# A linear-attention and gMLP block: k^T v regrouped as (x^T k) Wv, accumulated while tokens arrive, with some first layernorms on ScalarE and another order of loads

## The chip, the core and the metric

The kernel runs on one NeuronCore of a Trainium2 chip. The metric is the device time of one execution in microseconds, lower is better. Beside it stand profiles: each is one profiled execution, with the span from its first to its last instruction.

## What is computed

One token sequence, S = 2048 tokens of D = 512 channels in bf16, passes through two blocks:

```python
h  = x + A(layernorm(x))          # linear attention, 32 heads of 16 channels
h2 = h + B(layernorm(h))          # gMLP, F = 1792, Fh = 896

# A: q, k, v = x @ wqkv;  phi(t) = (t + 1 if t > 0 else exp(t)) + 1e-6
kv  = einsum('bhsd,bhse->bhde', phi(k), v);   z = einsum('bhsd->bhd', phi(k))
o   = (phi(q) @ kv) / (phi(q) . z + 1e-6);    A = o @ wo
# B: z1, z2 = halves of gelu(x @ w_in)
g   = w_sp @ layernorm(z2) + b_sp;            B = (z1 * g) @ w_out
```

Only the products of channels within one head count in kv, so the 512 x 512 product of phi(k) and v is masked to blocks of 16. Since v = x Wv for the normalised x, the product k^T v can also be written by way of x^T k and Wv.

## The kernel before

The 2048 tokens are 16 tiles of 128 (NT), taken in 8 pairs (NP). Everything stays in SBUF. The eight PSUM banks (2 KB per partition each) are handed out by a pool, `PS`, one bank or an aligned run of banks at a time; a pool slot is free again when the last operation on its tile has ended.

The program is a list of operations (`op`), each with an engine, a planned cost, a priority and the operands that it reads and writes. `Program.schedule` (L185) plays this list through with the planned costs and fixes the order of each engine's queue and the buffer slots: each engine takes the operation that could start soonest, within a small patience, and among those the one of the lowest priority number. `NUDGE` (L372) is a table of numbers added to the priorities, one for each operation. At run time the order of each queue (PE, ACT, DVE, POOL, SP) is fixed, with semaphore waits where `_waits` (L274) found a dependence. DMAs are issued by the queues of SP, ACT and POOL; on POOL each DMA also waits until the one before it has landed.

The stages, by line:

- Loads (L539 to L552): tile 0 by SP, tile 1 by ACT, wk in two halves, the other tiles in pairs, wv and wq by SP. wo, win and wout by POOL: wo after tile 5 is normalised (L657), wout after the q projections of L743 (L744), win after the seventh pair's phi(k) (L719). w_sp is transposed by DMA on SP's queue as time permits (L554), 26 of 64 pieces early.
- Warm-up of PE: eight matmuls on zeros (L603), in a PSUM bank of their own.
- First layernorm (L643): statistics (L610, L614) on DVE, the root by Ln and Exp on ACT (L624, L626), the normalisation on DVE (L638) into a pool of four tiles, `XN`.
- Transposes of the normalised tiles into xT: pairs 0 to 2 on PE (L676) with an evacuation by ACT (L681), the others by DMA on SP's queue (L665). `XDMA` = 3 is that border.
- For each pair the projections k and v (L708, each 8 matmuls of 512 columns into two banks). phi(k): Exp on ACT (L687), min on DVE (L688), max on DVE (L695), into pk. v: evacuated by ACT (L722), beside two columns of ones.
- q projections (L734) for groups of four tiles, with the same phi, into pqT. The fourth group comes after the tokens (L857).
- k^T v (L757): for each of four channel blocks 16 matmuls of 130 columns, accumulated over the token tiles; the columns of ones give z. Then on DVE a copy of z (L769), the mask (L775) and a transpose (L777). The product with wo (L787) is evacuated by DVE and ACT (L795, L792) into mw.
- Denominators (L807 to L814), their spreading (L824, L846) and scaling of pqT (L850), then y = pq mw (L879), the residual (L884), the second layernorm.
- Stage B: win (L907 for z2, L952 for z1), the token mixing (L982) and the output projection (L1000), all on PE.

Of the kernel before, what the change touches and what calls it, by code (L numbers as in the profile page):

```python
# [5 lines left out]
FP32 = mybir.dt.float32  # L6
# [103 lines left out]
class Program:  # L110
# [293 lines left out]
def bass_sequential_preLN__linear_attn_block__mixer_gmlp__prompt_kernel(  # L404
# [18 lines left out]
    VS = 136  # L423
# [20 lines left out]
    pk_b, v_b = NT * D * 2, NT * KD * VS * 2  # L444
    s_kv = Store(nc, "pk_v_z2", pk_b + v_b)
    s_xn = Store(nc, "xn", 4 * D * 2)
# [17 lines left out]
    v = View(s_kv, pk_b, [NT, KD, VS], BF16)  # L464
    gz2 = View(s_kv, 0, [NT, FH], BF16)
    mw = View(s_kv, NT * FH * 2, [KD, D], BF16)

# [20 lines left out]
    mhalf = small([TPG], FP32)  # L488

# [7 lines left out]
    xn_v = View(s_xn, 0, [4, D], BF16)  # L497
# [43 lines left out]
    load("act", "x1", x[1, :], x_dram[P:2 * P, :], P * D * 2, prio=-20)  # L541
    for c in (0, 2):
        load("sp", "wk", wk[c:c + 2, :], w3[:, c:c + 2, D:2 * D], D * D + (170000 if c == 0 else 0), whole=True, prio=c / 2 + 1)

    def load_x(p, prio):
        load("sp", f"x{p + 1}", x[2 * p:2 * p + 2, :],
             x_dram[2 * p * P:(2 * p + 2) * P, :].rearrange("(n p) d -> p n d", p=P), 2 * P * D * 2, prio=prio)

    for p in range(1, NP):
        load_x(p, 2 + p)  # L550
    load("sp", "wv", wv.all(), w3[:, :, 2 * D:3 * D], D * D * 2, prio=2.5 + WV)
    load("sp", "wq", wq.all(), w3[:, :, 0:D], D * D * 2, prio=2 + NP)  # L552

    def load_wsp(tg, sts, after=()):  # L554
# [186 lines left out]
    for gq in range(NQ1):  # L741
        for f in (0, 2):
            o = q_proj(gq, f, Q0 - 5 + gq)  # L743
# [331 lines left out]
```

## Time and profile before

| | us |
|---|---|
| median of 3 runs | 253.16 (252.9 to 253.57) |
| the profiled execution's own time | 253.07 |
| its span | 251.3 |
| PE busy, share of the span | 240.3, 96% |
| DVE busy | 137.4, 55% |
| ACT busy | 82.1, 33% |
| POOL busy | 24.5, 10% |

In the profile PE is TensorE's matmuls, PEld its weight loads, DVE is VectorE, ACT is ScalarE, POOL is GpSimd, SP is SyncE; a q behind the name is the engine's queue of DMA issues. L12 is line 12 of the kernel. A group gives its line, engine, operation, output<-inputs, shapes, count, then busy time, mean time of one in ns, idle time of the engine just before, and who ended it. Buffers that share a store have one name: xT_pq_z is xT, pqT and z1T; pk_v_z is phi(k), v, mw and z2; wqkv_wsp is wq, wk, wv, wo and later part of w_sp. [...]

### The profile page before, as it was taken

To read this page: it belongs to the slowest core of one execution; us is meant where nothing else is said; L and a number is where in the kernel's file an instruction comes from. 1 tells how busy PE (TensorE), PEld (TensorE's weight loads), DVE (VectorE), ACT (ScalarE), POOL (GpSimd) and SP (SyncE) were. 2 spreads that over 40 slices of the span, in tenths; PEclk is the share of its full clock that TensorE was granted. 3 is DMA by queue.
4 is the path that set the end of the run, shared out by engine and by line. 5 is a ranking of instruction groups with operands and counts; after the bars stand their busy time and mean duration, and the time that the engine had idled before them with its cause. 6 is when DMAs were issued, how large, how long until landed. Compare 5 with 4: busy or idle time off the path is not lost.

```text
span 251.3 us, 3084 instructions
## 1 busy us (share of the span) xinstructions
PE 240.3 (96%) x1204; PEld 110.7 (44%) x1204; DVE 137.4 (55%) x265; ACT 82.1 (33%) x115; POOL 24.5 (10%) x65
## 2 busy tenths in 40 slices
PE   5879989998999999999999999999999999999995
PEld 1434434473344444444444444444444444444442
DVE  2888897677999989905233223343313523323443
ACT  3638456638965666686920000000010000000000
POOL 7300000110020352412300000000000000000000
PEclk9999999999999999999999999999999999999999
DMA  6994644799301230435444444211000110000022
GB/s 196 357 220 104 93 99 104 188 234 257 100 5 36 42 69 17 86 84 93 97 105 103 87 104 104 63 41 45 0 0 3 42 42 0 0 3 0 0 83 83
DMA packets 54782, 21.30 MB, mean 85 GB/s; under 512 B 48400, under 2 KB 54032, under 8 KB 54768
## 3 DMA queue, kind: packets, MB, share of 16 engines
q1 hardware_dynamic: 53968, 17.71, 31.7%
q0 software_dynamic: 656, 3.28, 4.1%
q8 instruction: 9, 0.15, 0.3%
q10 hardware_dynamic: 144, 0.13, 0.2%
q14 instruction: 5, 0.04, 0.1%
HBM read 7.47 MB, written 2.10 MB: 38 GB/s over the span
## 4 chain that ended last, share of the span: by engine, by line
PE 84%; DVE 6%; DMA 5%; SPq 2%; ACT 1%; issue 1%
PE ps L982 38%; PE ps L907 10%; PE ps L1000 10%; PE ps L952 10%; PE ps L708 6%; PE ps L734 5%; PE ps L879 4%; DMA wqkv_wsp<-in_A_wqkv_dram 4%; SPq L536 2%; DVE xT_pq_z L695 2%; PE ps L757 1%; DVE xT_pq_z L850 1%; DMA xT_pq_z<-xn 1%; ACT e L687 1%; DVE small L610 1%
## 5 line engine op out<-in xcount | busy, mean ns | idle before, releaser
L982 PE MATMUL ps<-wsp,pk_v_z 128*128 128x512 bf16 x336 | 73.2, 379 | 0.0
L988 DVE TENSOR_TENSOR r<-ps,e 128x512 bf16<-128x512 f32 x28 | 19.4, 691 | 67.5 <-PE ps L982 67.5
L982 PEld LDWEIGHTS ps<-wsp,pk_v_z 128*128 128x128 bf16 x336 | 32.9, 98 | 39.7
L957 ACT ACTIVATE xT_pq_z<-ps 128x1024 bf16<-128x1024 f32 x14 | 14.2, 1023 | 62.1 <-PE ps L952 61.9
L708 PE MATMUL ps<-wqkv_wsp,xT_pq_z 128*128 128x512 bf16 x128 | 29.3, 379 | 0.9 <-ACT xT_pq_z L681 0.5
L907 PE MATMUL ps<-win,hT 128*128 128x512 bf16 (+1 forms) x128 | 25.7, 353 | 0.4 <-ACT hT L681 0.4
L952 PE MATMUL ps<-hT,win 128*128 128x512 bf16 x112 | 25.2, 379 | 0.0
L1000 PE MATMUL ps<-wout,xT_pq_z 128*128 128x512 bf16 x112 | 24.7, 379 | 0.0
L982 PE MATMUL ps<-wqkv_wsp,pk_v_z 128*128 128x512 bf16 x112 | 24.3, 379 | 0.0
L610 DVE BATCH_NORM_STATS2 small<-xh 128x6 f32<-128x512 bf16 x32 | 20.9, 679 | 4.6 <-DMA xh<-in_A_x_dram 4.5
L687 ACT ACTIVATE e<-ps 128x1024 bf16<-128x1024 f32 x16 | 16.1, 1023 | 13.1 <-PE ps L708 8.0
L708 PEld LDWEIGHTS ps<-wqkv_wsp,xT_pq_z 128*128 128x128 bf16 x128 | 12.1, 98 | 16.5 <-ACT xT_pq_z L681 1.2
L907 PEld LDWEIGHTS ps<-win,hT 128*128 128x128 bf16 x128 | 12.4, 98 | 13.0 <-ACT hT L681 0.7
L916 ACT ACTIVATE pk_v_z<-ps 128x896 bf16<-128x896 f32 x16 | 14.5, 915 | 10.9 <-PE ps L907 10.8
L734 PE MATMUL ps<-xT_pq_z,wqkv_wsp 128*128 128x512 bf16 x64 | 15.5, 379 | 2.5 <-DMA wqkv_wsp<-in_A_wqkv_dram 1.6
L1006 DVE TENSOR_TENSOR r<-ps,xh 128x512 bf16<-128x512 f32 x16 | 11.1, 691 | 11.7 <-PE ps L1000 11.7
L982 PEld LDWEIGHTS ps<-wqkv_wsp,pk_v_z 128*128 128x128 bf16 x112 | 11.0, 98 | 13.2
L1000 PEld LDWEIGHTS ps<-wout,xT_pq_z 128*128 128x128 bf16 x112 | 11.0, 98 | 13.2
L952 PEld LDWEIGHTS ps<-hT,win 128*128 128x128 bf16 x112 | 11.0, 98 | 12.8
L879 PE MATMUL ps<-pk_v_z,xT_pq_z 128*128 128x512 bf16 x64 | 15.2, 379 | 0.6 <-DVE xT_pq_z L850 0.5
L931 DVE BATCH_NORM_STATS2 small<-pk_v_z 128x6 f32<-128x512 bf16 (+1 forms) x16 | 9.8, 619 | 9.6 <-ACT pk_v_z L916 9.4
L638 DVE TENSOR_SCALAR xn<-xh,small 128x512 bf16<-128x512 bf16 x32 | 12.0, 408 | 1.9 <-DMA xT_pq_z<-xn 1.2
(68 smaller groups left out, 173.5 us busy)
## 6 DMA issues: line engine op xcount, KB each, us to landing
out_dram<-r SPq DMA_DIRECT2D x16, 128.0 KB, 1.7
xh<-in_A_x_dram SPq DMA_DIRECT2D x7, 256.0 KB, 6.6
win<-in_B_w_in_dram POOLq DMA_DIRECT2D x1, 1792.0 KB, 9.8
wqkv_wsp<-in_A_wqkv_dram SPq DMA_DIRECT2D x2, 512.0 KB, 7.7
wout<-in_B_w_out_dram POOLq DMA_DIRECT2D x1, 896.0 KB, 6.2
wsp<-in_B_w_sp_dram SPq DMA_TRANSPOSE x48, 2.8
wqkv_wsp<-in_A_wqkv_dram SPq DMA_DIRECT2D x2, 256.0 KB, 4.0
wqkv_wsp<-in_A_wo_dram POOLq DMA_DIRECT2D x1, 512.0 KB, 8.8
```

The lines of the kernel that those rows point to most:

```text
L610: op("dve", dve_c(512), lambda e: e.bn_stats(s6.ap(), src.ap()), r=[src], w=[s6], prio=prio)
L687: op("act", act_c(1024), lambda e: e.activation(e_().ap(), t(flat).ap(), ACT.Exp), r=[t()], w=[e_()], prio=prio)
L708: i = e.matmul(t(bank(ti)).ap(), lhsT=lhs.ap()[:, c, :], rhs=rhs.ap()[:, c, :], start=(c == 0), stop=(c == KD - 1))
L734: r_ = e.matmul(t(bank(i)).ap(), lhsT=lhs.ap()[:, c, :], rhs=rhs.ap()[:, c, :], start=(c == 0), stop=(c == KD - 1))
L879: i = e.matmul(t(bank(ti)).ap(), lhsT=l.ap()[:, c, :], rhs=mw[c, :].ap(), start=(c == 0), stop=(c == KD - 1))
L907: k = e.matmul(t(bank(i)).ap()[:, 0:b - a], lhsT=l.ap()[:, c, :], rhs=win[c, a:b].ap(), start=(c == 0), stop=(c == KD - 1))
L916: op("act", act_c(FH, ptr=by_act), lambda e, t=t, d=d, acc={"accum_out": m.ap()} if by_act else {}: e.activation(d.ap(), t(flat).ap()[:, 0 ...
L952: k = e.matmul(t(bank(i)).ap(), lhsT=l.ap()[:, c, :], rhs=r_.ap()[:, c, :], start=(c == 0), stop=(c == KD - 1))
L957: op("act", act_c(1024), lambda e: e.activation(d.ap(), t(None if same else flat).ap(), ACT.Gelu_apprx_tanh), r=[t()], w=[d], prio=prio, a ...
L982: k = e.matmul(t(bank(0)).ap(), lhsT=l.ap()[:, s - a, :], rhs=r_.ap()[:, s - a, :], start=(s == 0), stop=(s == NT - 1))
L988: op("dve", dve_c(512), lambda e: e.tensor_tensor(gb().ap(), t(bank(0)).ap(), bsp().ap()[:, tg * GW:(tg + 1) * GW], ALU.add), r=[t(), bsp( ...
L1000: k = e.matmul(t(bank(0)).ap(), lhsT=l.ap()[:, fc, :], rhs=wout[fc, :].ap(), start=(fc == 0), stop=(fc == KF - 1))
```

## The change

- v is no longer projected. From each tile's normalised x (lhsT) and phi(k) (rhs), four matmuls of 512 columns add to x^T k in four PSUM banks, `acc`, held from the warm-up (which now writes there) to the end of the tokens. Their priority is 10p + `KA`, KA = 35.
- After the tokens x^T k is copied to SBUF (half by ACT, half by DVE), multiplied by Wv (16 matmuls of 128 columns), and masked straight into kvmT; the two DVE transposes go. z comes from 16 matmuls of a block of 32 ones columns with phi(k), on four strips of output columns, a copy by ACT and four matmuls of two columns.
- All 16 normalised tiles have places of their own (`xn`, where v was). Of tiles 4 to 15, those with n % 4 >= `NA` = 1 are normalised by ACT (Identity with scale and bias per partition; DVE makes the bias).
- Tile 1 is loaded by SP after tile 0, then tiles 2 and 3; half of wk by ACT, behind the memset of the warm-up operand; wq after tiles 8 and 9, wv last. wo is loaded after tile 12's normalisation instead of tile 5's.
- Pair 2 is transposed by DMA too (`XDMA` = 2). The first three q groups have priority 20gq + `QI`, QI = 15. `NUDGE` has other numbers throughout.

```diff
-    WARM, XDMA, HDMA, LNACT = 8, 3, 1, 2
-    WV = 2
+    WARM, XDMA, HDMA, LNACT = 8, 2, 1, 2
+    WV, WQ, NA, KA, QE, QI = 8.5, 4, 1, 35, 3, 15
...
-    load("act", "x1", x[1, :], x_dram[P:2 * P, :], P * D * 2, prio=-20)
-    for c in (0, 2):
-        load("sp", "wk", wk[c:c + 2, :], ..., D * D + (170000 if c == 0 else 0), whole=True, prio=c / 2 + 1)
...
+    load("sp", "x1", x[1, :], x_dram[P:2 * P, :], P * D * 2, prio=1)
+    for p in range(1, NP):
         load("sp", f"x{p + 1}", ..., 2 * P * D * 2, prio=1 + p)
+    load_wk = [load(e, "wk", wk[c:c + 2, :], ..., D * D + 60000, whole=True, prio=q)
+               for e, c, q in (("act", 0, -20), ("sp", 2, 2.5))]
+    load("sp", "wv", wv.all(), w3[:, :, 2 * D:3 * D], D * D * 2, prio=1.5 + WV)
+    load("sp", "wq", wq.all(), w3[:, :, 0:D], D * D * 2, prio=1.5 + WQ)
...
-    idle = Tile(PS)
+    acc = Tile(PS, KD)
...
+        by_act = [n for n in grp if n >= 4 and n % 4 >= NA]
+        if by_act:
+            nb = small([len(grp)], FP32)
+            op("dve", 0.11, lambda e, nb=nb, m=m, rs=rs: e.scalar_tensor_tensor(
+                nb.all().ap(), m.ap(), -1.0, rs.all().ap(), op0=ALU.mult, op1=ALU.mult), ...)
         for i, n in enumerate(grp):
+            if n in by_act:
+                o = op("act", act_c(512, ptr=1), lambda e, d=d, n=n, a=a, c=c: e.activation(
+                    d.ap(), x[n, :].ap(), ACT.Identity, bias=c.ap(), scale=a.ap()), ...)
+            else:
+                o = normalise(d, x[n, :], Row(st_x, n), 6, rs[i:i + 1], 10 * (n // 2) - 18)
+            if n == 12:
+                load("pool", "wo", ...).deps[o] = True
...
-        t = kv_proj(p, wv, 10 * p + 1)
-        op("act", act_c(1024), ..., r=[t()], w=[d], prio=10 * p + 1)
+        for n in (2 * p, 2 * p + 1):
+            l, r_ = xn[n, :], pk[n, :]
+            def mm(e, n=n, l=l, r_=r_):
+                for c in range(KD):
+                    i = e.matmul(acc(bank(c)).ap(), lhsT=l.ap()[:, c * P:(c + 1) * P], rhs=r_.ap(), start=(n == 0),
+                                 stop=(n == NT - 1))
+            op("pe", 4 * MM, mm, r=[l, r_], w=[acc()], prio=10 * p + KA)
...
-            o = q_proj(gq, f, Q0 - 5 + gq)
+            o = q_proj(gq, f, 20 * gq + QI if gq < QE else Q0 - 5 + gq)
...
+    zp, zs, zt = Tile(PS), Tile(XN), Tile(PS)
+        for n in range(NT):
+            a = 32 * (n % 4)
+            i = e.matmul(zp(bank(0)).ap()[a:a + 32, :], lhsT=ones.all().ap(), rhs=pk[n, :].ap(), start=(n < 4),
+                         stop=(n >= NT - 4))
...
+    op("act", act_c(512), lambda e: e.activation(zs().ap(), zp(bank(0)).ap(), ACT.Copy), ..., prio=Q0 + 2)
+            i = e.matmul(zt(bank(0)).ap()[:, 2 * c:2 * c + 2], lhsT=zs().ap()[:, c * P:(c + 1) * P], rhs=part.all().ap(), ...)
...
+        if h == 0:
+            op("act", act_c(1024), lambda e, d=d, s=s: e.activation(d.ap(), s.ap(), ACT.Copy), ..., prio=Q0 + 2)
+        else:
+            op("dve", dve_c(1024), lambda e, d=d, s=s: e.tensor_copy(d.ap(), s.ap()), ..., prio=Q0 + 2)
+        for c in range(KD):
+            for j in range(KD):
+                i = e.matmul(vk(bank(0)).ap()[:, c * P:(c + 1) * P], lhsT=wv.ap[:, j, c * P:(c + 1) * P],
+                             rhs=xtk.ap[:, j, c * P:(c + 1) * P], start=(j == 0), stop=(j == KD - 1))
+    op("dve", dve_c(512), lambda e: e.tensor_tensor(kvmT()..., vk(bank(0))..., bmask..., ALU.mult), ..., prio=Q0 + 2)
```

More of the change, by code (lines that the diff above doesn't have):

```diff
@@ L488, in bass_sequential_preLN__linear_attn_block__mixer_gmlp__prompt_kernel @@
     mhalf = small([TPG], FP32)
+    ones = small([32], BF16)
+    part = small([2], BF16)
     psum = nc.alloc_psum_tensor("ps", [P, 8, 512], FP32)
@@ L565, in bass_sequential_preLN__linear_attn_block__mixer_gmlp__prompt_kernel @@
     warm = zeros.all()
-    op("pool", 0.3, lambda e: e.memset(warm.ap(), 0.0), w=[warm], prio=-9)
+    load_wk[0].deps[op("pool", 0.3, lambda e: e.memset(warm.ap(), 0.0), w=[warm], prio=-9)] = True
     op("pool", 0.2, lambda e: e.memset(ident.all().ap(), 0.0), w=[ident.all()])
@@ new lines, in bass_sequential_preLN__linear_attn_block__mixer_gmlp__prompt_kernel, with mm @@
+    zp, zs, zt = Tile(PS), Tile(XN), Tile(PS)
+    def mm(e):
+        for n in range(NT):
+            a = 32 * (n % 4)
+            i = e.matmul(zp(bank(0)).ap()[a:a + 32, :], lhsT=ones.all().ap(), rhs=pk[n, :].ap(), start=(n < 4),
+                         stop=(n >= NT - 4))
+        return i
+    op("pe", 1.1, mm, r=[pk.all(), ones.all()], w=[zp()], prio=Q0 + 1.5)
+    op("act", act_c(512), lambda e: e.activation(zs().ap(), zp(bank(0)).ap(), ACT.Copy), r=[zp()], w=[zs()], prio=Q0 + 2)
+    def mm(e):
+        for c in range(KD):
+            i = e.matmul(zt(bank(0)).ap()[:, 2 * c:2 * c + 2], lhsT=zs().ap()[:, c * P:(c + 1) * P], rhs=part.all().ap(),
+                         start=True, stop=True)
+        return i
@@ new lines, in bass_sequential_preLN__linear_attn_block__mixer_gmlp__prompt_kernel, with sums @@
+    op("pe", 0.25, mm, r=[zs(), part.all()], w=[zt()], prio=Q0 + 2)
+    d = zc[:, 0:HC]
+    def sums(e, d=d):
+        m = bmask.ap.rearrange("p (a h e) -> p a h e", a=1, e=DH)[:, :, :, 0].to_broadcast([P, KD, HC])
+        s = zt(bank(0)).ap()[:, 0:2 * KD].rearrange("p (c f) -> p c f", f=2)[:, :, 0:1]
+        return e.tensor_tensor(d.ap(), m, s.to_broadcast([P, KD, HC]), ALU.mult)
+    op("dve", 0.15, sums, r=[zt(), bmask.all()], w=[d], prio=Q0 + 2)
+    for h in range(2):
+        d = xtk[2 * h:2 * h + 2, :]
+        s = acc(lambda v, h=h: v[:, 2 * h:2 * h + 2, :])
+        if h == 0:
+            op("act", act_c(1024), lambda e, d=d, s=s: e.activation(d.ap(), s.ap(), ACT.Copy), r=[s], w=[d], prio=Q0 + 2)
+        else:
+            op("dve", dve_c(1024), lambda e, d=d, s=s: e.tensor_copy(d.ap(), s.ap()), r=[s], w=[d], prio=Q0 + 2)
@@ new lines, in bass_sequential_preLN__linear_attn_block__mixer_gmlp__prompt_kernel, with mm @@
+    vk, kvmT = Tile(PS), Tile(XN)
+    def mm(e):
+        for c in range(KD):
+            for j in range(KD):
+                i = e.matmul(vk(bank(0)).ap()[:, c * P:(c + 1) * P], lhsT=wv.ap[:, j, c * P:(c + 1) * P],
+                             rhs=xtk.ap[:, j, c * P:(c + 1) * P], start=(j == 0), stop=(j == KD - 1))
+        return i
+    op("pe", 16 * 0.058, mm, r=[wv.all(), xtk.all()], w=[vk()], prio=Q0 + 2)
+    op("dve", dve_c(512), lambda e: e.tensor_tensor(
+        kvmT().ap().rearrange("p (c f) -> p c f", c=KD), vk(bank(0)).ap().rearrange("p (c f) -> p c f", c=KD),
+        bmask.ap.rearrange("p (a f) -> p a f", a=1).to_broadcast([P, KD, P]), ALU.mult),
+       r=[vk(), bmask.all()], w=[kvmT()], prio=Q0 + 2)
```

79 lines of the change are left out of this document (24 added, 55 removed), and 53 rows, old and new, of the table NUDGE.

## The prediction

> **What bounds the kernel now.** I read the first part of the page, then busy time by stretch, the chain that ended last, and TensorE's waits.
>
> ```profile
> span 251.3 us, 3084 instructions
> PE 240.3 (96%) x1204; PEld 110.7 (44%) x1204; DVE 137.4 (55%) x265; ACT 82.1 (33%) x115; POOL 24.5 (10%) x65
> ```
> ```profile
> 0.00:6.58 6.58, 3.60 (x9) 1.04 (x9) 2.05 (x6) 2.06 (x5) 4.74 (x22) 1.00 0.70 201
> 6.58:25.34 18.76, 16.19 (x88) 7.32 (x89) 15.90 (x39) 11.64 (x18) 1.68 (x4) 1.00 0.88 224
> 25.34:50.87 25.53, 24.67 (x113) 10.88 (x114) 20.65 (x33) 14.16 (x16) 0.95 (x1) 1.00 0.59 124
> 50.87:67.32 16.45, 15.07 (x136) 8.00 (x135) 12.91 (x22) 11.16 (x15) 0.79 (x1) 1.00 0.94 216
> 67.32:248.43 181.11, 180.73 (x860) 83.46 (x860) 85.24 (x168) 43.03 (x63) 16.36 (x38) 1.00 0.21 48
> 248.43:251.30 2.87, 0.00 (x0) 0.00 (x0) 0.69 (x1) 0.00 (x0) 0.00 (x0) 1.00 0.27 91
> ```
>
> The columns of the second view are the stretch, its length, then PE, PEld, DVE, ACT, POOL busy, the clock, DMA share, GB/s. From 67.32 to 248.43 PE is busy 180.73 of 181.11 us: that part is solid matmul work, and no line of it is in the diff. So the time is a sum: when PE's real work starts, plus its work, plus its idle time before 67.32, plus fixed parts. Whatever the change does to the moment 67.32 is carried to the end one for one, as long as stage B's inputs keep up. PE's idle time is 2.57 us in the early stretch (18.76 - 16.19), 0.86 in the middle one, 1.38 in the tail.
>
> ```profile
> PE ps L734 <- DMA wqkv_wsp<-in_A_wqkv_dram: 1.6, 1, 1.6
> PE ps L734 <- DVE xT_pq_z L695: 0.7, 1, 0.7
> ```
>
> The largest single wait after the start is L734 (q) for the DMA of wq: 1.6 us, in the early stretch.
>
> **The change part by part.** *PE work.*
>
> ```profile
> 41.37 9.50 PE ps L708 x44
> 52.59 3.63 PE ps L757 x64
> 57.08 0.33 PE ps L807 x4
> 69.22 0.24 PE ps L676 x4
> ```
>
> These are rows of the chain (start, length, what, count). A 512-wide matmul is 9.50 / 44 = 0.216 us. Of L708's 128 matmuls the 64 for v go (13.8 us); x^T k brings 64 of the same width (4 per token tile, 16 tiles): 13.8 us, net nothing. The k^T v block, L757, goes: -3.63. The third pair is transposed by DMA, so 8 PE transposes go: 2 x 0.24 = -0.48. Added: Wv against x^T k, 16 matmuls of 128 columns, at L757's 3.63 / 64 = 0.057: 0.91. Four 2-column matmuls that turn the sums: at most 4 x 0.057 = 0.23. And 16 matmuls of 512 columns on 32 output columns each (the sums of pk). No row shows those sixteen; the nearest is L807, four such matmuls on four different column strips, 0.33 us for the four, where one after another they would take 0.86. Bounds: 4 x 0.216 = 0.86 if the four strips overlap fully, 16 x 0.216 = 3.46 if not at all; I take 1.1, a little under 4 x 0.33. Sum: -3.63 - 0.48 + 0.91 + 0.23 + 1.1 = **-1.87 us**. [...]
>
> *Start.*
>
> ```profile
> 0.80 0.39 SPq L536 DMA_DIRECT2D xh<-in_A_x_dram  x1
> 0.80 0.40 ACTq L536 DMA_DIRECT2D xh<-in_A_x_dram  x1
> 1.23 1.28 ACT L596 ACT_TABLE_LOAD   x1 [1.23 <-PEq L1060]
> 3.82 1.29 DVE L610 BATCH_NORM_STATS2 small<-xh 128x6 f32<-128x512 bf16 x2 [3.82 <-DMA xh<-in_A_x_dram]
> 7.35 1.29 DVE L610 BATCH_NORM_STATS2 small<-xh 128x6 f32<-128x512 bf16 x2 [0.43 <-DMA xh<-in_A_x_dram]
> 7.66 2.99 PE L708 MATMUL ps<-wqkv_wsp,xT_pq_z 128*128 128x512 bf16 x12 [0.29 <-ACT xT_pq_z L681]
> 7.41 0.47 SPq L536 DMA_DIRECT2D wqkv_wsp<-in_A_wqkv_dram  x1
> ```
>
> Token tile 1 moves from ACT's queue to second on SP, so it lands about one issue (0.4 us) later; half of wk moves from SP to ACT, behind the wait for a memset and the 1.28 us table load, so it is issued near 2.1 instead of 1.24. The first layernorm chain can then run for tile 0 alone instead of both tiles' statistics first: up to 0.65 earlier (half of 1.29). Bounds of the first k matmul (7.66 now): 0.8 earlier to 0.4 later. I take **-0.4**.
>
> *Early stretch.* Tiles 2 and 3 are issued third on SP instead of fourth behind wk; their statistics start at 7.35 now, after a wait for the DMA. wq is last on SP today, issued at 7.41, and moves ahead of the last two pairs and of wv, which are not needed then. With that the 1.6 us wait goes. What is late next is a PSUM slot: x^T k holds four of the eight banks from the first instruction on, so only two double-bank slots are left for k and q (four before).
>
> ```profile
> 15.75 1.23 DVE L695 SCALAR_TENSOR_TENSOR pk_v_z<-ps,e 128x1024 bf16<-128x1024 f32 x1
> 50.70 1.89 PE L734 MATMUL ps<-xT_pq_z,wqkv_wsp 128*128 128x512 bf16 x8
> 52.63 1.02 ACT L687 ACTIVATE e<-ps 128x1024 bf16<-128x1024 f32 x1 [0.70 <-PE ps L734]
> 53.69 0.43 DVE L688 TENSOR_SCALAR e<-e 128x1024 bf16<-128x1024 bf16 x1 [1.77 <-ACT e L687]
> 54.15 1.23 DVE L695 SCALAR_TENSOR_TENSOR xT_pq_z<-ps,e 128x1024 bf16<-128x1024 f32 x1
> ```
>
> A clean tile holds its slot from 50.70 to 55.38: 4.68 us (matmuls, exp, min, max). The very first k tile is held from 7.66 to 16.98, because DVE does statistics first. I expect PE to lose about 1.6 us in the early stretch instead of 2.57 (bounds 0.6 to 4): **-1.0**.
>
> *Middle stretch.* The x^T k matmuls need no slot of their own and rank (KA = 35) three pairs behind, so they are what PE does while the slots are full. PE work per k or q tile here is (64 + 64 + 48) x 0.216 / 14 = 2.71 us; two slots deliver one tile per half a holding time, so PE stays fed while the mean holding time is under 5.4 us. DVE and ACT decide that:
>
> ```profile
> 3.82:51.93 48.11, 43.07 (x209) 18.84 (x208) 39.65 (x76) 27.60 (x38) 5.14 (x13) 1.00 0.74 174
> ```
> ```profile
> L638 DVE TENSOR_SCALAR xn<-xh,small 128x512 bf16<-128x512 bf16 x32 | 12.0, 408 | 1.9 <-DMA xT_pq_z<-xn 1.2 <-ACT small L626 0.7
> L923 ACT ACTIVATE r<-pk_v_z,small 128x896 bf16<-128x896 bf16 x8 | 8.3, 1044 | 1.1 <-POOL small L921 1.1
> L722 ACT ACTIVATE pk_v_z<-ps 128x1024 bf16<-128x1024 f32 x8 | 8.2, 1024 | 4.1 <-PE ps L708 4.1
> ```
>
> DVE is busy 39.65 of 48.11 us in the token phase, ACT 27.60. Nine normalisations (tiles 5, 6, 7, 9, 10, 11, 13, 14, 15) move to ACT: DVE loses 9 x 0.41 = 3.7 and gains three tiny products. ACT loses eight evacuations of v, 8.2, and gains nine normalisations; of the 128x512 kind no row stands, so between 0.6 (1044 x 512 / 896) and 1.04, I take 0.7: +6.3. Both engines get lighter. Behind a waiting ACT normalisation on ACT's queue stands the next exp, and a k or q slot waits for that, at worst the 0.7 itself. [...]
>
> I leave the middle idle time as it is (bounds -0.5 to +4): **0**.
>
> SP's queue: two more transposes of xn, and those of tiles 4 and 5 now lie ahead of PE's third pair.
>
> ```profile
> 37.21 1.37 DVE L638 TENSOR_SCALAR xn<-xh,small 128x512 bf16<-128x512 bf16 x4
> 70.13 1.69 PE L907 MATMUL ps<-win,hT 128*128 128x512 bf16 x8 [0.36 <-ACT hT L681]
> 73.99 2.54 SPq L665 DMA_TRANSPOSE hT<-xn  x2
> 51.69 0.79 POOL L536 DMA_DIRECT2D win<-in_B_w_in_dram  x1 [5.55 <-DMA wout<-in_B_w_out_dram]
> win<-in_B_w_in_dram POOLq DMA_DIRECT2D x1, 1792.0 KB, 9.8
> wqkv_wsp<-in_A_wo_dram POOLq DMA_DIRECT2D x1, 512.0 KB, 8.8
> ```
>
> A transpose takes SP 1.27 us, the two 2.54; SP has until 73.99 before the first hT transpose, so they cost nothing unless tiles 4 and 5 come later than PE's work on tiles 0 to 3 lasts. That work is some 11 us (k and x^T k for two pairs, 6.9; the first q group, 3.5; transposes, 0.5). On POOL's queue wo moves behind tile 12's normalisation, and wout and win follow one by one: win lands now at 51.69 + 9.8 = 61.5. If tile 12 is normalised at 37, as now (the four at 37.21), and wo takes 8.8, and wout as long as now, win lands near 63, and the first use (70.13 now) would be near 67. Covered; if tile 12 came at 42 it would not be.
>
> *Tail.* Before, k^T v, a mask, two DVE transposes (0.45 each) and wo follow the last pk. Now the last x^T k, an evacuation split over ACT and DVE, Wv, one mask, wo.
>
> ```profile
> 58.38 0.45 PE ps L787 x2
> 58.85 1.23 DVE L795 CAST pk_v_z<-ps 128x1024 bf16<-128x1024 f32 x1 [1.60 <-PE ps L787]
> L988 DVE TENSOR_TENSOR r<-ps,e 128x512 bf16<-128x512 f32 x28 | 19.4, 691 | 67.5 <-PE ps L982 67.5
> ```
>
> From the last x^T k: 1.23 (as L795), 0.91 on PE, 0.69 (as L988), wo 0.45 for the first half, 1.23, with some 0.6 of handovers: 5.1 us until the first y (L879, at 62.32 now). What covers it on PE: the fourth q group, 16 x 0.216 = 3.46, the sums, 1.3, Wv and wo themselves, 1.8, the denominators. This is enough, but DVE's order may not be ideal; idle 1.7 instead of 1.38: **+0.3** (bounds -0.3 to +2.6).
>
> *Sum:* -1.87 - 0.4 - 1.0 + 0 + 0.3 = -2.97. Against the profiled execution's own 253.07 (span 251.3 and 1.77 around it), which lies 0.09 under the median 253.16, this gives **250.1 us**.
>
> **The rivals.**
>
> *A, slower: two PSUM slots are too few.* Place: the token phase. It decides from a mean holding time of 5.4 us on. Against it: 4.68 for a clean tile, and a lighter DVE and ACT. For it: the first tile's 9.3, and DVE's 82% share (39.65 of 48.11), since statistics stand in the same in-order queue. If the fourteen tiles hold 6.5 us each, one comes per 3.25, 0.54 over PE's 2.71: 14 x 0.54 = 7.6 us, of which the x^T k and q work left for the end gives about 1 back: +6.6, **256.7**. [...]
>
> *B, about the same: the chain behind the last x^T k is bare.* If DVE takes the fourth q group's min and max (2 x 1.66) ahead of the evacuation and the mask, the full upper bound of the tail falls due: 2.6 instead of 0.3: **252.4**.
>
> *C, more: idle time before the tail nearly vanishes.* The x^T k backlog fills every hole, and the start gains its 0.8: early idle 0.6, middle 0.4, which is 1.9 more than in the forecast: **248.2**.
>
> *D, the sums' matmuls don't overlap:* 3.46 instead of 1.1: **252.5**. L807's row speaks against it.
>
> **How the numbers follow.** Forecast 0.53, A 0.18, B 0.13, C 0.12, D 0.04. A measurement of this kernel tells about 0.3%, 0.76 us, from no change. The forecast and C lie below 252.4, with part of B: faster 0.70. Rest of B and D, and the lightest form of A: same 0.11. A: slower 0.19. The range takes in C and its last bound (-0.5 in the middle, another -0.3 in the tail) below, 247.4, and above B, D and the milder half of A, 254.6.
>
> **What would show it.** Right: L757's group gone, a new group of 64 512-wide matmuls, one of 16 with a total near 1 us, and the first y matmul about 3 us earlier than 62.32; no wait for wq; PE's idle time before stage B near 4.5 us. Wrong: PE waits for the max on DVE (the slot's releaser) in the token phase, many times, by several us in total (A); DVE casts or masks as PE's releaser in the tail (B); transposes of xn as PE's releaser early on; win or wo landing after PE could use it.

## The result, and the profile after

| | before | after |
|---|---|---|
| median of 5 runs each, us | 253.45 (252.9 to 253.81) | 250.58 (250.06 to 251.89) |
| ratio, 95% interval | | 0.9906 (0.9887 to 0.9925) |
| the profiled execution, us | 253.07 | 250.06 |

The changed kernel is 0.9% faster, 2.9 us by the medians and 3.01 us between the two profiled executions; the forecast was 250.1. In a later group of runs it had 251.27 (250.67 to 251.68, 6 runs), a ratio of 0.9923 (0.9907 to 0.9939). The sum of the prediction is right. Its terms are not all right, and the first two views show where.

The first part of the page after:

```profile
span 248.3 us, 2993 instructions
PE 236.6 (95%) x1146; PEld 108.0 (43%) x1168; DVE 135.8 (55%) x256; ACT 81.9 (33%) x117; POOL 25.7 (10%) x66
```

Busy time by stretch after. The stretches end where PE has done the same wide matmuls as in the view of before: 64 in the first; in the second 8 more, because half of the fourth q group now comes before the tail; the third ends where sixteen matmuls of y are done.

```profile
6.12:24.55 18.43, 15.57 (x79) 6.84 (x81) 16.85 (x39) 12.11 (x19) 1.24 (x5) 1.00 0.81 208
24.55:51.56 27.01, 26.23 (x122) 11.58 (x127) 18.75 (x28) 13.46 (x16) 2.85 (x3) 1.00 0.70 148
51.56:64.15 12.59, 11.29 (x100) 5.26 (x101) 10.08 (x15) 10.56 (x14) 0.00 (x0) 1.00 0.94 251
64.15:245.40 181.25, 179.93 (x845) 83.23 (x860) 86.82 (x170) 43.60 (x63) 17.30 (x38) 1.00 0.23 49
```

Stage B begins at 64.15 instead of 67.32, 3.17 us earlier, and lasts 181.25 instead of 181.11: what is gained before it arrives at the end. (Matmul records are missing here and there, x845 against x860 in the last row, so that differences of busy time below 0.3 us mean little; the lengths are exact.) With 8 x 0.216 = 1.73 us of q counted back to the tail, the gain splits like this:

| part | forecast | measured, us | from |
|---|---|---|---|
| PE's real work starts | -0.4 | -0.46 | 6.58 to 6.12 |
| early stretch | -0.48 - 1.0 | -0.33 | 18.76 to 18.43 |
| middle | 0 | -0.25 | 25.53 to 27.01 - 1.73 |
| tail | -1.39 + 0.3 | -2.13 | 16.45 to 12.59 + 1.73 |

The early stretch gave 1.15 us less than forecast, the tail 1.04 more. PE's waits after:

```profile
PE ps L690 <- DVE pk_xn_z L638: 1.8, 2, 1.2
PE ps L722 <- DMA xT_pq_z<-pk_xn_z: 1.4, 4, 0.6
PE ps L752 <- ACT xT_pq_z L695: 1.3, 1, 1.3
PE ps L818 <- DVE hn L807: 0.7, 1, 0.7
```

The wait for wq is gone, as forecast. In its place stand other waits: for transposes by DMA (1.4 in four pieces), and 1.3 for ACT's evacuation of the second pair's transposes (0.25 before, in front of the L708 group at 12.23). PE's timeline of the start (start, length, what, and in brackets the idle time ahead of it with its releaser) shows how:

```profile
6.12 0.40 PE L690 MATMUL ps<-small,pk_xn_z 128*128 128x128 bf16 x4 [1.15 <-DVE pk_xn_z L638]
7.12 0.40 PE L690 MATMUL ps<-small,pk_xn_z 128*128 128x128 bf16 x4 [0.60 <-DVE pk_xn_z L638]
7.36 1.94 PE L722 MATMUL ps<-wqkv_wsp,xT_pq_z 128*128 128x512 bf16 x8
9.43 0.62 PE L690 MATMUL ps<-small,pk_xn_z 128*128 128x128 bf16 x8
11.33 1.90 PE L752 MATMUL ps<-xT_pq_z,wqkv_wsp 128*128 128x512 bf16 x8 [1.28 <-ACT xT_pq_z L695]
19.00 1.02 PE L722 MATMUL ps<-wqkv_wsp,xT_pq_z 128*128 128x512 bf16 x4 [0.59 <-DMA xT_pq_z<-pk_xn_z]
```

Before, v of pair 0 followed k of pair 0 at once, because it needs only xT, and PE had that to do while pair 1 was prepared. Its replacement x^T k needs phi(k), which needs exp, min and max first, so after k and the transposes of pair 1 PE has nothing to do until the evacuation has ended. This is read from the two timelines; no run tests it by itself. ACT's queue at that time:

```profile
9.33 1.02 ACT L701 ACTIVATE e<-ps 128x1024 bf16<-128x1024 f32 x1 [1.13 <-PE ps L722]
10.26 1.02 ACT L695 ACTIVATE xT_pq_z<-ps 128x1024 bf16<-128x1024 bf16 x1
```

The exp of the first k runs from 9.33, the evacuation follows at 10.26, and PE goes on at 11.33. The exp ahead of it costs little: the transposes themselves end at 10.05 (9.43 + 0.62), and the evacuation takes 1.02.

The waits for DMA in the early stretch (0.59 at 19.00, and 0.20 at 20.23) are for tiles 4 and 5, the third pair, which PE itself transposed before. SP's queue shows where they come from:

```profile
7.29 9.01 SPq L557 DMA_TRANSPOSE wsp<-in_B_w_sp_dram  x6
16.34 5.19 SPq L679 DMA_TRANSPOSE xT_pq_z<-pk_xn_z  x4
```

Tile 4 is normalised by 13.27 (DVE, 12.87 + 0.40), but its transpose is issued at 16.34, behind six transposes of w_sp that are needed much later.

The tail after, on PE:

```profile
51.49 1.05 PE L770 MATMUL ps<-pk_xn_z,small 128*32 128x512 bf16 x16
54.31 1.05 PE L803 MATMUL ps<-wqkv_wsp 128*128 128x128 bf16 x16
55.30 0.83 PE L838 MATMUL ps<-xT_pq_z,zc 128*32 128x512 bf16 x12
56.78 0.81 PE L818 MATMUL ps<-wqkv_wsp,hn 128*128 128x512 bf16 x3 [0.65 <-DVE hn L807]
59.41 1.04 PE L910 MATMUL ps<-pk_xn_z,xT_pq_z 128*128 128x512 bf16 x4
```

The sixteen matmuls of sums take 1.05 by the profile, and 0.98 until the next PE work: the four strips overlap, since sixteen 512-wide matmuls one after another would take 3.46. The mask (L807) costs PE 0.65. The first y is at 59.41 instead of 62.32.

### The profile page after: what moved, and what is told of

It is laid out like the page before. It is cut to its first block, busy times and chain, and to the rows that moved or that the text cites. A ratio compares the mean times of both kernels' runs of the same rounds, so it can differ in the third digit from the quotient of the medians.

```text
span 248.3 us, 2993 instructions
## 1 busy us (share of the span) xinstructions
PE 236.6 (95%) x1146; PEld 108.0 (43%) x1168; DVE 135.8 (55%) x256; ACT 81.9 (33%) x117; POOL 25.7 (10%) x66
## 4 chain that ended last, share of the span: by engine, by line
PE 84%; DVE 6%; DMA 5%; ACT 2%; SPq 1%; issue 1%
PE ps L1013 39%; PE ps L983 10%; PE ps L938 10%; PE ps L1031 10%; PE ps L910 5%; PE ps L722 4%; PE ps L739 3%; DMA xT_pq_z<-pk_xn_z 3%; PE ps L752 2%; DMA xh<-in_A_x_dram 2%; DVE small L610 2%; ACT e L701 2%; DVE xT_pq_z L709 1%; DVE xT_pq_z L881 1%; SPq L540 1%
## 5 line engine op out<-in xcount | busy, mean ns | idle before, releaser
L1013 PE MATMUL ps<-wsp,pk_xn_z 128*128 128x512 bf16 x328 | 72.9, 379 | 0.4
L1013 PEld LDWEIGHTS ps<-wsp,pk_xn_z 128*128 128x128 bf16 x336 | 32.9, 98 | 39.6
L938 PE MATMUL ps<-win,hT 128*128 128x384 bf16 (+1 forms) x124 | 25.8, 352 | 0.6 <-issue 0.4
L1013 PE MATMUL ps<-wqkv_wsp,pk_xn_z 128*128 128x512 bf16 x110 | 24.2, 379 | 0.1
L947 ACT ACTIVATE pk_xn_z<-ps 128x896 bf16<-128x896 f32 x16 | 14.6, 917 | 13.3 <-PE ps L938 12.6
L1013 PEld LDWEIGHTS ps<-wqkv_wsp,pk_xn_z 128*128 128x128 bf16 x112 | 10.9, 98 | 13.2
L722 PE MATMUL ps<-wqkv_wsp,xT_pq_z 128*128 128x512 bf16 x64 | 15.3, 379 | 1.4 <-DMA xT_pq_z<-pk_xn_z 1.4
L910 PE MATMUL ps<-pk_xn_z,xT_pq_z 128*128 128x512 bf16 x64 | 15.1, 379 | 0.4 <-DVE xh L915 0.3
L739 PE MATMUL ps<-pk_xn_z 128*128 128x512 bf16 x60 | 14.9, 379 | 0.2
L1022 DVE TENSOR_TENSOR xT_pq_z<-xT_pq_z,r 128x512 bf16<-128x512 bf16 x28 | 11.9, 425 | 1.0
```

Of the source, the lines that this page charges most:

```text
L722: i = e.matmul(t(bank(ti)).ap(), lhsT=lhs.ap()[:, c, :], rhs=rhs.ap()[:, c, :], start=(c == 0), stop=(c == KD - 1))
L739: i = e.matmul(acc(bank(c)).ap(), lhsT=l.ap()[:, c * P:(c + 1) * P], rhs=r_.ap(), start=(n == 0), stop=(n == NT - 1))
L910: i = e.matmul(t(bank(ti)).ap(), lhsT=l.ap()[:, c, :], rhs=mw[c, :].ap(), start=(c == 0), stop=(c == KD - 1))
L938: k = e.matmul(t(bank(i)).ap()[:, 0:b - a], lhsT=l.ap()[:, c, :], rhs=win[c, a:b].ap(), start=(c == 0), stop=(c == KD - 1))
L947: op("act", act_c(FH, ptr=by_act), lambda e, t=t, d=d, acc={"accum_out": m.ap()} if by_act else {}: e.activation(d.ap(), t(flat).ap()[:, 0 ...
L1013: k = e.matmul(t(bank(0)).ap(), lhsT=l.ap()[:, s - a, :], rhs=r_.ap()[:, s - a, :], start=(s == 0), stop=(s == NT - 1))
```

## The experiments

The theory to test, T: the gain is PE work that is no longer done (k^T v out, overlapped sums in), carried to the end one for one; loads and normalisations on ScalarE add a little at the start, and two PSUM slots are enough because they are held less than the edge of 5.4 us. The rivals: the gain is in the other edits and the regrouping is worth little; or the slots bind. They ran in three groups, each on one chip beside the kernel before (medians 253.12, 253.11 and 253.2): the first four, the four without priority tables, and the four on the start. The changed kernel itself stands only in the third group, so the first four are held against it by their ratios to the kernel before. All four profiles of that group start late (first transposes at 6.77, 8.52, 7.06 and 7.18, against 6.12 and 6.50 in the two profiles of after), also where the edit leaves the start alone. Their medians can contain some of that; a stretch of one profile held against the same stretch of another does not.

**one_strip**: the sixteen matmuls of sums all on one strip of output columns, the order of all queues kept.

```diff
-            a = 32 * (n % 4)
-            i = e.matmul(zp(bank(0)).ap()[a:a + 32, :], lhsT=ones.all().ap(), rhs=pk[n, :].ap(), start=(n < 4),
-                         stop=(n >= NT - 4))
+            a = 0
+            i = e.matmul(zp(bank(0)).ap()[a:a + 32, :], lhsT=ones.all().ap(), rhs=pk[n, :].ap(), start=(n == 0),
+                         stop=(n == NT - 1))
...
```

The copy of the sums and the matmuls that turn them then read that one strip.

> The changed kernel with the sixteen matmuls of the sums all on one strip of 32 output columns, so that they can't overlap; the order of every queue is that of the changed kernel. First theory (the time is a sum of TensorE's work up to stage B, and whatever that work gains or loses arrives at the end one for one): the group takes 16 x 0.216 = 3.5 instead of 1.0 us and the kernel gets 2.5 us slower, about 253.0. Rival (the gain came from earlier loads and a lighter VectorE, and the tail is a chain through evacuation, mask and denominators in which TensorE has time to spare): under 0.8 us slower, about 251.

Measured 253.81 (8 runs), ratio 1.002 (1.0007 to 1.0033): by the two measurements of after (0.9906 and 0.9923) 2.5 to 2.9 us slower. Its tail:

```profile
52.86 3.63 PE L770 MATMUL ps<-pk_xn_z,small 128*32 128x512 bf16 x16
63.49 1.02 PE L910 MATMUL ps<-pk_xn_z,xT_pq_z 128*128 128x512 bf16 x4
```

The group takes 3.63 instead of 1.05, and from its start to the first y pass 10.63 us instead of 7.92: 2.58 more work, 2.71 more time. The profiled executions differ by 4.04 (254.1 and 250.06): 1.37 had been lost before the group began, at the start, and 2.71 in the tail. Work on PE in the tail is paid in full, so the prediction's method of summing it holds. Rival D of the prediction has its price here too, about 2.7: without the overlap most or all of the gain would be lost.

**f_old_loads**: the loads in the order and on the queues of before; the other queues keep the order of after.

```diff
...
+        order["sp"][:] = [by["x0"][0], k0, k1, by["x2"][0], by["x3"][0], by["wv"][0]] + [
+            by[f"x{i}"][0] for i in (4, 5, 6, 7, 8)] + [by["wq"][0]] + rest
+        order["act"][:] = by["x1"] + [o for o in order["act"] if o is not k0]
+        k0.deps = {}
...
```

> The changed kernel with the loads of x, wk, wv and wq issued in the order and by the queues of the kernel before; every other queue keeps its order, and wo stays where the change put it. First theory (loads are worth the early start and the wait for wq, the rest of the gain is TensorE's work): between 1 and 3 us slower, near 252.5, with a wait for wq at the first q group that is in the trace. Rival (the loads were hidden anyway): within 0.4 us of the changed kernel, 250.6.

Measured 252.97 (251.92 to 254.16, 12 runs), ratio 0.9992 (0.9974 to 1.001): 1.7 to 2.2 us slower than after by the ratios. The reason is not the wait for wq, which the prediction had named for the loads. No such wait shows; the q matmuls of the first group wait for ACT instead. PE simply starts late, by DVE's and PE's timelines:

```profile
7.46 0.69 DVE L613 BATCH_NORM_STATS2 small<-xh 128x6 f32<-128x512 bf16 x1 [2.52 <-DMA xh<-in_A_x_dram]
8.07 0.40 DVE L641 TENSOR_SCALAR pk_xn_z<-xh,small 128x512 bf16<-128x512 bf16 x1
```
```profile
8.52 0.60 PE L693 MATMUL ps<-small,pk_xn_z 128*128 128x128 bf16 x4 [3.56 <-DVE pk_xn_z L641]
9.90 3.62 PE L725 MATMUL ps<-wqkv_wsp,xT_pq_z 128*128 128x512 bf16 x8
```

In DVE's queue the statistics of tile 2 stand ahead of the normalisation of tile 0. With wk loaded before tiles 2 and 3, DVE waits 2.52 us for tile 2, and tile 0, long ready, waits behind it. The old loads hurt here also because DVE's order was made for the new ones, so this is not the worth of the loads alone.

**f_dve_norm**: the nine normalisations that ACT does go back to DVE, inserted in its queue by their planned start.

```diff
...
+            def f(e, n=n):
+                return e.tensor_scalar(xn[n, :].ap(), x[n, :].ap(), Row(st_x, n)[6:7].ap(), rss[n].ap(),
+                                       op0=ALU.subtract, op1=ALU.mult)
+            o.fn = f
+            order["act"].remove(o)
+            at = [i for i, q in enumerate(order["dve"]) if q.start >= o.start][0]
+            order["dve"].insert(at, o)
...
```

> The changed kernel with the nine normalisations that ScalarE took given back to VectorE, each where its planned start puts it in VectorE's queue; all other orders are kept. First theory (VectorE has room, its work is hidden behind TensorE): 0 to 0.8 us slower, about 250.9. Rival (the relief of VectorE is what pays): 1.5 us slower or more, 252 or above, with slots of k and q held longer and TensorE waiting for the max on VectorE.

Measured 251.99 (251.18 to 254.4, 12 runs), ratio 0.9966 (0.9945 to 0.9988): 1.1 to 1.5 us slower than the two measurements of after (0.9923, 0.9906), between what the theory and the rival had. From the first q to the first y, by busy time in the stretch, the two kernels stand like this, f_dve_norm first, then after:

```profile
14.09:61.70 47.61, 45.76 (x253) 20.42 (x253) 37.96 (x68) 21.60 (x28) 2.77 (x3) 1.00 0.73 169
```
```profile
11.33:59.41 48.08, 45.54 (x248) 20.36 (x253) 36.00 (x59) 28.14 (x37) 2.85 (x3) 1.00 0.76 174
```

DVE has 37.96 us to do instead of 36.00, and the stretch is no longer, 47.61 against 48.08. What the profiled execution lost, it lost before the first q (14.09 instead of 11.33), where the edit changes nothing. So this profile does not show a price of DVE's load; where the 1.1 to 1.5 us of the medians come from stays open, and the late starts of this group are one candidate.

**exp_twice**: each exp of phi is done twice, which changes no value and holds each PSUM slot about 1 us longer (an exp takes 1.02).

```diff
+            e.activation(e_().ap(), t(flat).ap(), ACT.Exp).then_inc(twice[0], 1)
+            done.append(0)
+            e.wait_ge(twice[0], len(done))
+            return e.activation(e_().ap(), t(flat).ap(), ACT.Exp)
...
```

> The changed kernel with each of the sixteen Exp of k and q done twice, the second waiting for the first, so that a PSUM slot is held about 1.1 us longer (4.7 to 5.8); orders are kept, ScalarE gets 17 us more. First theory (two slots deliver a tile per half a holding time, and TensorE needs one per 2.7 us, so that 5.4 us is the edge): beyond the edge by 0.4, so 14 x 0.2 = 2.8 us slower, 1.5 to 5, about 253.4. Rival (the x^T k matmuls that wait in line cover a late slot): under 0.6 us slower, about 251.

Measured 259.63 (5 runs), ratio 1.0257 (1.0235 to 1.028), 8.9 us over after: several times what I had expected. PE's timeline in the middle, and PE's waits:

```profile
30.52 1.90 PE L758 MATMUL ps<-xT_pq_z,wqkv_wsp 128*128 128x512 bf16 x8 [0.47 <-DVE pk_xn_z L715]
32.26 1.89 PE L745 MATMUL ps<-pk_xn_z 128*128 128x512 bf16 x8
34.62 1.90 PE L758 MATMUL ps<-xT_pq_z,wqkv_wsp 128*128 128x512 bf16 x8 [0.47 <-DVE pk_xn_z L715]
37.29 1.90 PE L728 MATMUL ps<-wqkv_wsp,xT_pq_z 128*128 128x512 bf16 x8 [0.77 <-DVE xT_pq_z L715]
```
```profile
PE ps L758 <- ACT xT_pq_z L696: 2.5, 1, 2.5
PE ps L758 <- DVE pk_xn_z L715: 1.8, 4, 0.5
PE ps L728 <- DVE xT_pq_z L715: 1.0, 2, 0.8
PE ps L728 <- DVE pk_xn_z L715: 0.8, 1, 0.8
```

The max on DVE (L715), the last reader of a slot, now releases PE again and again. A slot that is taken at 30.52 is taken next at 37.29, 6.8 us later. The stretch from the first q to the first y, to be held against 48.08 us in after:

```profile
14.94:69.82 54.88, 48.88 (x253) 20.16 (x253) 36.13 (x59) 42.93 (x52) 2.71 (x3) 0.97 0.63 141
```

It is 6.8 us longer, but not all of that is the slots. PE's idle time there is 6.0 (54.88 - 48.88) against 2.5 in after: the waits for the max add up to 4.0 (3.6 in the lines above, the rest in small ones), the wait for the mask grows from 0.65 to 1.48, and the waits for transposes by DMA are gone. The other 3.3 us are busy time for the same matmuls; 1.7 of them are the first two groups, which took 3.19 and 2.33 instead of 1.90 and 1.89; the mean granted clock of the stretch is 0.97, against 1.00 in after. The rest of the busy time I can't put down.

Another 3.6 us are the start, where the first q comes at 14.94 instead of 11.33:

```profile
8.40 3.45 PE L728 MATMUL ps<-wqkv_wsp,xT_pq_z 128*128 128x512 bf16 x8
14.94 3.19 PE L758 MATMUL ps<-xT_pq_z,wqkv_wsp 128*128 128x512 bf16 x8 [2.52 <-ACT xT_pq_z L696]
```

Of these, 2.2 are there before the first exp can matter: the transposes of tile 0 come 1.06 later and the first k matmuls run at half rate (3.45 instead of 1.94). The remaining 1.4 are mostly the evacuation of pair 1, which stands behind two exps (a wait of 2.52 instead of 1.28). Together that is the 10.4 us between the two profiled executions (260.47 and 250.06).

So rival A's mechanism is real: a slot held too long makes PE wait. Its price is somewhat smaller than A had it. From 14.94 to 55.79 a slot is taken again after 5.8 to 7.1 us, 6.3 on average; by A's sum that makes 14 x (3.15 - 2.71) - 1 = 5.2 us, and the waits for the max are 4.0. My expectation for this run, 1.5 to 5 us, holds for the waits for slots alone; what it had left out is the start, the clock and the mask. In the changed kernel no wait for the max stands among PE's largest.

**Without the priority tables.** NUDGE was made for each kernel separately, so the parts of the change can be taken apart only where it is left out (`g.schedule()`). Four kernels: before and after without it; the regrouping alone (x^T k, the sums and their tail on before's loads, DVE normalisations, XDMA = 3, wo after tile 5); and all but the regrouping (v and k^T v as before; loads, ScalarE normalisations, places for the normalised tiles, XDMA = 2, QI and wo as in the change).

> The kernel before with its table of added priorities left out (all zero), so that the planner orders by the written priorities alone. It is the base for the three kernels beside it: slower than the kernel before by some per cent, 255 to 262. A theory that the whole difference between the two kernels lies in these tables would have it as fast as the changed kernel without its table.

> The changed kernel with its table of added priorities left out. First theory (the gain is TensorE's work and the start): 2 to 4 us under the kernel before without its table. Rival (the gain lies in the new numbers of the table): within 1 us of it, or above.

> The regrouping alone, without tables: x^T k, the sums and Wv as in the changed kernel, but loads, wo, normalisations, the third pair's transposes and the priorities of q as before. First theory: TensorE's work falls by 1.4 us (the 0.5 of the transposes stays), some of it lost because x^T k has to wait for phi(k) early on: 0.5 to 1.5 us under the kernel before without its table. Rival (regrouping is neutral or bad by itself, four banks are missing): equal or slower by up to 4 us.

> Everything but the regrouping, without tables: the kernel before with the new order of loads, nine normalisations on ScalarE, places for all sixteen normalised tiles, wo after tile 12, the third pair transposed by DMA and the new priorities of q; v and k^T v as before. First theory: start and early idle time gain about 1 us, the rest nothing: 0.5 to 1.5 us under the kernel before without its table. Rival (this half is the whole gain): 2.5 to 4 us under it.

| without NUDGE, median us (ratio to the kernel before) | v projected, k^T v | x^T k |
|---|---|---|
| other edits as before | 265.11 (1.0475) | 267.93 (1.0581) |
| other edits as after | 257.8 (1.0172) | 255.15 (1.0092) |

By the medians the regrouping alone costs 2.8 us; with the other edits it gains 2.65 (257.8 - 255.15). The other edits gain 7.3 without it. The rival had the direction right: the regrouping alone is not faster. The other three lie outside what was expected of them: n0_before above 262, n0_after 10 us under it instead of 2 to 4, and all but the regrouping 7.3 under it instead of 0.5 to 1.5 (first theory) or 2.5 to 4 (rival).

Most of the difference between +2.8 and -2.65 goes with TensorE's clock, though. In the profiled executions the mean granted clock is 0.981 (n0_before), 0.974 (the regrouping alone), 0.987 (all but the regrouping) and 1.000 (n0_after), over spans of 263.4, 266.2, 256.1 and 253.4 us. As an estimate, the missing share of the clock times the span is 5.0, 6.9, 3.3 and 0 us; n0_before's timeline has slow matmuls: sixteen for k at 27.18, behind a wait of 3.42 us, take 5.04, the sixteen at 12.77 take 3.63. Without these amounts the regrouping would cost some 0.9 us by itself and 0.7 beside the other edits: the PE work that it saves can't be seen in either column. What it is worth in the tuned kernel can only be read from the two profiles: 2.13 us gained in the tail, about 1.0 lost to the longer wait for the second pair's evacuation (1.28 against 0.25).

The largest wait, in PE's timeline of the regrouping alone:

```profile
28.90 3.57 PE L735 MATMUL ps<-wqkv_wsp,xT_pq_z 128*128 128x512 bf16 x8 [4.77 <-DVE small L619]
```

One wait of 4.77 us, and the eight matmuls behind it then run at half rate, 3.57 instead of 1.9. The profile puts the wait down to DVE's statistics, which these matmuls do not read; late transposes of their tiles or a late slot are possible, and which it was stays open. These kernels have no tuned order, so the 7.3 is not the worth of the other edits in the real one; there, f_old_loads says 1.7 to 2.2 for the loads, with the reserve made above.

**The start.** The last group asks why one and the same kernel scatters by 1.8 us (250.06 to 251.89). after_again is the changed kernel; norm_first puts DVE's normalisations of tiles 0 and 1 ahead of the statistics of tile 2; warm_12 has 12 warm-up matmuls instead of 8; norm_first_warm has both.

```diff
+        first = [o for o in order["dve"] if o in norms]
+        rest = [o for o in order["dve"] if o not in norms]
+        order["dve"][:] = rest[:4] + first + rest[4:]
...
-        for _ in range(WARM):
+        for _ in range(12):
```

> The changed kernel once more, as the base of the three beside it on the same chip, and for a second profile of its first ten microseconds. Theory: VectorE's queue holds the normalisation of tile 0 behind the statistics of tile 2, so the landing of tiles 2 and 3 sets when TensorE starts; where TensorE has by then idled 1.8 us or more, its first k matmuls run at half rate (0.43 us each). So the runs scatter between 250 and 252, and the profile has either a first k near 7.4 at full rate or one past 8 at half rate, with a total some 2 us apart. Rival: the start is the same in each run, and the scatter has other reasons.

> The changed kernel with the normalisations of tiles 0 and 1 put ahead of the statistics of tile 2 in VectorE's queue; all other orders are kept. Theory: TensorE's first transposes come at 5.6 or before whatever the DMA of tiles 2 and 3 does, the first k near 6.5 at full rate, and about 1 us is gained: 249.6, with less scatter. Rival (pair 1, which needs tiles 2 and 3, sets the pace anyway): within 0.4 us of the changed kernel.

> The changed kernel with twelve warm-up matmuls instead of eight, orders kept. Theory: TensorE is busy until about 6, so that its first k matmuls run at full rate also where the tiles come late: 0.5 to 1 us gained in the median, 249.8. Rival (the rate of the first matmuls doesn't follow the idle time before them): no change, or slower where the warm-up is still running when the tiles are there.

> Both of the former: normalisations of tiles 0 and 1 first, twelve warm-up matmuls. Theory: the first transposes come right behind the warm-up, near 5.8, the first k near 6.7 at full rate in every run: 1 to 1.5 us gained, 249.3. Rival: within 0.4 us of the changed kernel, 250.6.

| | median us (range) | ratio, interval |
|---|---|---|
| after_again | 251.27 (250.67 to 251.68) | 0.9923 (0.9907 to 0.9939) |
| norm_first | 250.41 (250.21 to 251.37) | 0.99 (0.9883 to 0.9916) |
| warm_12 | 250.79 (250.32 to 250.97) | 0.9899 (0.9883 to 0.9915) |
| norm_first_warm | 250.55 (250.44 to 250.91) | 0.9901 (0.9887 to 0.9915) |

PE's timeline of after_again, and its busy time up to the first q (the third number from the right, 0.75, is the granted clock):

```profile
6.50 0.40 PE L690 MATMUL ps<-small,pk_xn_z 128*128 128x128 bf16 x4 [1.86 <-DVE pk_xn_z L638]
7.48 0.56 PE L690 MATMUL ps<-small,pk_xn_z 128*128 128x128 bf16 x4 [0.58 <-DVE pk_xn_z L638]
7.83 3.46 PE L722 MATMUL ps<-wqkv_wsp,xT_pq_z 128*128 128x512 bf16 x8
13.31 1.90 PE L752 MATMUL ps<-xT_pq_z,wqkv_wsp 128*128 128x512 bf16 x8 [1.58 <-ACT xT_pq_z L695]
```
```profile
6.50:13.31 6.81, 4.64 (x24) 2.23 (x25) 5.43 (x16) 3.68 (x7) 0.94 (x4) 0.75 1.19 347
```

And the same first k in warm_12 and in norm_first:

```profile
7.61 1.94 PE L722 MATMUL ps<-wqkv_wsp,xT_pq_z 128*128 128x512 bf16 x8
```
```profile
5.78 0.82 PE L695 MATMUL ps<-small,pk_xn_z 128*128 128x128 bf16 x8 [0.82 <-DVE pk_xn_z L641]
8.87 1.04 PE L727 MATMUL ps<-wqkv_wsp,xT_pq_z 128*128 128x512 bf16 x4 [0.96 <-ACT xT_pq_z L700]
```

In after_again PE stood idle 1.86 us after the warm-up instead of 1.15, and the first eight k matmuls took 3.46 us instead of 1.94. Of the 2.0 us by which the first q is later (13.31 against 11.33) 1.1 arrive at the end (the profiled executions are 251.17 and 250.06); one reason is that the third pair's transposes are in time for a PE that comes later (its k starts at 20.23 without a wait), so that the 0.79 us of waiting for them falls away. The two profiles of this kernel thus show one start at full rate and one at half; that the scatter of all its runs comes from there is not shown. In the profiles with four more warm-up matmuls, and with the earlier normalisation, the rate is full. Both single edits and the pair lie 0.5 to 0.9 us under after_again, but none is apart from the first measurement of after (0.9906). norm_first has the lowest median of all, 250.41; its interval still touches that of after_again, so that it is not shown to be faster than the changed kernel. The totals expected for the three (249.6, 249.8 and 249.3) were not reached, and the pair adds nothing to norm_first. Its gain of 0.3 us at the first transposes is partly lost to a new wait of 0.96 for ACT's evacuation, which now stands behind the roots of tiles 2 and 3.

## Why the prediction was right, and which step of it failed

- **PE work, -1.87: right.** The terms at the tail came as worked out: the sums 0.98 against 1.1, Wv about 1.0 against 0.91. one_strip shows that such work is paid one for one (2.58 us more work, 2.71 more time). With some 0.1 for the turn of the sums they make -1.56, against -1.39. The tail gained another 0.5 beside these terms and its idle time, which I can't put down to a line; its other matmuls are the same, but stand in fewer pieces (the denominators' sixteen in two groups instead of three, the q matmuls unbroken).
- **Tail idle, +0.3: wrong by 0.4.** Idle time there is 12.59 - 11.29 = 1.30, against 1.38 before. The chain of casts, Wv and mask is covered by q and the denominators better than I took it; DVE does the mask right after the first min. Rival B did not come.
- **Start, -0.4: right in size.** -0.46 in the transposes, -0.30 in the first k (7.66 to 7.36), which is the mark that the prediction used. But not only by the earlier chain of tile 0: what sets it is the arrival of tile 2, whose statistics stand ahead of tile 0's normalisation. DVE after:

```profile
4.11 0.30 DVE L614 BATCH_NORM_AGGREGATE small<-small 128x2 f32<-128x6 f32 x2
5.05 0.69 DVE L610 BATCH_NORM_STATS2 small<-xh 128x6 f32<-128x512 bf16 x1 [0.64 <-DMA xh<-in_A_x_dram]
5.66 0.40 DVE L638 TENSOR_SCALAR pk_xn_z<-xh,small 128x512 bf16<-128x512 bf16 x1
```

  These statistics start at 5.05 and the first transposes at 6.12; in f_old_loads at 7.46 and 8.52. The distance is 1.07 and 1.06. norm_first puts tile 0 ahead and starts at 5.78.
- **Early idle, -1.0: the step that failed.** "With that the 1.6 us wait goes" is right. "What is late next is a PSUM slot" is wrong: idle time is 18.43 - 15.57 = 2.86 (less what missing records hide), not 1.6. No wait for a slot shows. What was late is xT: 1.28 us for the evacuation of the second pair, 0.79 for the DMA transposes of the third, and 0.60 for the normalisation of tile 1. The change takes v away from PE at the one place where v was the only work that needed nothing but xT, and what replaces it comes a whole phi later. The prediction counted v and x^T k as equal work, 13.8 us each, and so they are; it did not ask when the first of each can run. That account of the 1.28 us is argued from the two timelines. The 0.79 us are a term that the prediction put at nothing ("they cost nothing unless tiles 4 and 5 come later than PE's work on tiles 0 to 3 lasts"): it counted what SP has to do, not that w_sp's transposes stand ahead of these. The move of the third pair to DMA saved 0.48 us of PE work and cost 0.79 of waiting. One of the prediction's own signs of being wrong came true here: transposes of xn as PE's releaser early on. PE's idle time before stage B is 4.94 (2.86 + 0.78 + 1.30), against the 4.5 that it named as a sign of being right.
- **Middle, 0, and the slots: right.** Idle 27.01 - 26.23 = 0.78 against 0.86; no slot wait. The first k tile's slot is taken at 7.36 and free at 12.4, 5.0 us, later ones are held some 4.7 to 5.1, all under the edge of 5.4. Beyond the edge PE waits for slots, as rival A had it, for somewhat less than A's price (exp_twice: 4.0 us, by A's sum 5.2).
- **ScalarE's normalisations.** One takes 0.81 us, not the 0.7 that I took:

```profile
L665 ACT ACTIVATE pk_xn_z<-xh,small 128x512 bf16<-128x512 bf16 x9 | 6.9, 806 | 0.2 <-DVE small L657 0.2
```

  That is 0.40 over DVE's 0.408. In the time of the kernel the move back to DVE brings nothing that can be seen: f_dve_norm's median is above after's, and its profile shows no difference where the normalisations lie.
- **The sum, -2.97 against -3.01**, came out that close because the missing 1.15 us of the early stretch were made up by the tail (1.04) and the middle (0.25). So the nearness of the total is partly luck. With the early stretch as it was and the rest as forecast, it would have been 251.2. The lower end of the range, 247.4, takes the bound of the middle twice, once in C (idle 0.4 there) and once more as -0.5; taken once it is 247.9.

## What to carry to other kernels

When a product is regrouped, compare not only the work but what each piece needs before it can start: v needed xT alone and filled PE while the next pair was prepared, x^T k needs phi(k) and can't. In the queues of this kernel, which run in a fixed order, an operation that waited for a DMA, or one that was needed only later, held up a ready operation behind it (the statistics of tile 2 ahead of tile 0's normalisation, 2.52 us of waiting in f_old_loads; w_sp ahead of tile 4's transpose, whose input was ready at 13.27 and which was issued at 16.34); look for such a pair at the start of a kernel first, where little else covers it. Before a difference between two kernels is put down to a part of the change, hold their granted clocks and their starts beside it: in the four kernels without tables (granted clocks from 0.974 to 1.000), and in exp_twice (0.987, and a start 3.6 us later), a good part of the difference lay there.

## What the runs showed that I had not expected

- **The rate of TensorE's first matmuls.** In after the eight warm-up matmuls take 3.60 us, 0.43 each, twice the 0.216 of later ones; in after_again they take 3.26. Behind them two kinds of slow start show. In one_strip (idle 1.80), f_dve_norm (2.10), f_old_loads (3.56) and the regrouping alone without NUDGE (1.25) the transposes, too, are slow (0.60 for four where after takes 0.40, or 1.03 for eight), and eight k matmuls take 3.59 to 3.62:

```profile
6.77 0.61 PE L690 MATMUL ps<-small,pk_xn_z 128*128 128x128 bf16 x4 [1.80 <-DVE pk_xn_z L638]
8.18 3.62 PE L722 MATMUL ps<-wqkv_wsp,xT_pq_z 128*128 128x512 bf16 x8
```

  In three of these the granted clock shows no fall: it reads 1.00 from 6.50 to 13.31 in one_strip, and 1.000 over the spans of f_dve_norm and f_old_loads. It reads 1.00 in the slow warm-up as well (1.37 to 4.97 in after), so that column misses this kind; in all four the warm-up (3.60) and the transposes had been slow before. In after_again (1.86) and exp_twice (2.22) the first four transposes run at full rate, 0.40, and then eight k matmuls take 3.46 and 3.45. Here the granted clock is lower: 0.75 in the mean from 6.50 to 13.31 in after_again, and 0.987 over the span of exp_twice, against 0.999 over that of after. The length of the pause alone does not decide it: the kernel before has 1.61 and does its first twelve k matmuls in 2.99, the kernel before without NUDGE has 1.09 and needs 3.86. What does is not shown.
- **Four strips.** Sixteen 512-wide matmuls of 32 output columns took 0.98 us on four strips by the start of the next work, and about 3.56 on one (the next q starts at 56.42 there): 3.6 times. Both lie some 0.1 us above 16 x 0.216 = 3.46 or a quarter of it.
